# Attention scores with the mask added by TensorE, the maximum subtracted by VectorE, and one exponential per slot

## The chip, the core and the metric

The kernel runs on one core of a Trainium2 chip, as one launch. The metric is the device time in microseconds (us); smaller is better. The engines are TensorE (PE; its weight loads are listed as PEld), VectorE (DVE), ScalarE (ACT), GpSimd (POOL) and SyncE (SP, which issues most of the DMA transfers). They run their own streams in program order and wait for each other by semaphores. TensorE writes its results to PSUM, which VectorE and ScalarE read.

## The reference

The reference chains three parts. The change lies in the first; the other two are only named here.

```python
# attention: q, k, v are (2, 8, 768, 64); blocks of 32, a window of 16
k_sum = k.reshape(B, H, 24, 32, D).max(axis=3)
v_sum = v.reshape(B, H, 24, 32, D).mean(axis=3)
scores_l = scale * q @ k.T                       # kept where |i - j| < 16, else -1e9
scores_s = scale * q @ k_sum.T + log(32)         # 24 summary columns for each row
scores_all = concat([scores_l_masked, scores_s])
a = exp(scores_all - max(scores_all))            # per row
a = a / (sum(a) + 1e-9)
out = a @ concat([v, v_sum])
# then: a mixture of 8 experts (512 -> 1024 -> 512), one expert for each token,
# then: a feed-forward (512 -> 2048 -> 512) with g = h * cos(h)
```

## The kernel before

**Tiles of the attention.** Since the window is narrow, 64 tokens of queries see 96 tokens of keys (KW) and the 24 block summaries: 120 columns (KC) for each tile of 64 tokens. Two heads are worked on together (a pair), and half of the sequence at a time, six tiles: that is a slot. There are 8 pairs (two batches of four) and so 16 slots, numbered i; `p, odd = divmod(i, 2)`. In a slot each of the six tiles gives an array of 128 rows (64 queries of two heads) by 120 columns.

**A slot's work.** `attn_scores` (L255) multiplies on TensorE: the stationary operand is `qz`, in which the queries of the one head stand in rows 0 to 63 and those of the other in rows 64 to 127, in different columns, with zeros in the other two quarters, so that one product of 128 rows gives both heads. It needs `qz` to be cleared once (`clear_qz`) and to be filled in two halves (`prep_q`, L174: one copy on VectorE, one on ScalarE). The six products go to two banks of PSUM (tile `ps`, one buffer). VectorE adds the mask (L269: 0 within the window, -1e9 outside, log 32 on the summaries) into SBUF and takes the negative maximum of each row (L275). In odd slots the means of v for the next pair are also multiplied into a corner of `ps` (L238), and ScalarE copies them out (`evac_v`, L245). `attn_exp` (L278) does six exponentials on ScalarE, each with its own column of maxima as the bias. One slot later `attn_aT` transposes the exponentials on TensorE (L287) and ScalarE copies them to SBUF (L292); another slot later `attn_av` multiplies them with v (L303: half of the array's columns for each tile, 24 instructions), and VectorE divides by the sum (L309, L310, L312).

**What sets the order.** The attention is under a manual schedule: the loop over the slots (`for i in range(NH + 2)`) writes the instructions of all engines in the order in which they are issued, and the loads too (`load_raw` for q, k and v, `load_vw` for the windows of v, all on SP's queue). GpSimd and VectorE reorder the raw rows (`shuffle`, L168) and TensorE transposes them (`prep_k`, L207, with its maxima L215 and copy L198; `prep_q`, L177). Between the slots' pieces stands other work by a plan (`PLAN`, L46, run by `at(i, place)`): the routing of the first batch's tokens to experts (transposes L370 and their copies L373 and L375, logits L382, squares L402, the square root on GpSimd L462, positions and gates), the scatter of the rows to DRAM by expert (L538), the loading of the first window of tokens (L754, x_gate L760, x_first L774) and of the experts' weights. `ON_VECTOR` names copies that VectorE does in place of another engine. After the loop come the experts' windows and the feed-forward (all their products are at L716).

**The start.** The first k, q and v, then the constants `csa` (the mask among them), are loaded on SP's queue; TensorE multiplies zeros meanwhile (`keep_warm`, L1009).

Of the kernel before, what the change touches and what calls it, by code (L numbers as in the profile page):

```python
# [11 lines left out]
F32 = mybir.dt.float32  # L12
# [9 lines left out]
P = 128  # L22
# [39 lines left out]
# patterns times 2**16  # L62
# [3 lines left out]
# column offsets in the constant array  # L66
# [13 lines left out]
def shape_constants():  # L80
# [5 lines left out]
    m = np.zeros((P, NU + 1, KC), np.float32)  # L86
# [3 lines left out]
    m[:, :, :KW] = np.where(band, 0.0, -1e9)[:, None, :]  # L90
    m[:, 0, :WIN] = -1e9
    m[:, NU, KW - WIN:KW] = -1e9
    m[:, :, KW:] = math.log(BLK)
    c[:, C_MASK:C_MASK + (NU + 1) * KC] = m.reshape(P, -1)
# [9 lines left out]
def fused_kernel(ctx, tc, q, k, v, emb, tau, w1, w2, w_in, w_out, consts, out):  # L104
# [6 lines left out]
    # the second batch's rows and transposed rows; later a slot of weights  # L111
# [13 lines left out]
    mask = csa[:, C_MASK - C_VIND:C_TOK - C_VIND]  # L125
# [19 lines left out]
    def load_vw(b, g, half, vw):  # L145
        """the windows of half the sequence; those at its ends are short"""
# [16 lines left out]
    def shuffle(raw, n, scale, ap, eng, r=None):  # L163
        """raw [n, head, token, d] to [n, token, head, d]"""
        if r is None:
            r = ap.tile([P, QJ, 2, D], F32, tag="shuf", name="shuf", bufs=1)
        r = r[0:n]
        eng.tensor_scalar(  # L168
            r.rearrange("p j h d -> p h j d"), raw.rearrange("p h (j d) -> p h j d", d=D),
            scale, 1.0, op0=ALU.mult, op1=ALU.mult,  # L170
        )
        return r

    def prep_q(bf, qs, ps_t):  # L174
        pq = ps_t.tile([P, QJ, P], F32, tag="tr", name="pq")
        for j in range(QJ):
# [11 lines left out]
        tc.declare_no_dep(hi.ins, lo.ins, reason="different quadrants")  # L188
# [13 lines left out]
    def prep_k(bf, kr, pks, ap, eng, copy_first=False):  # L202
        """pks: a tile of PSUM, or two so that two engines can read them"""
# [32 lines left out]
    def prep_v2(va, pv):  # L236
        """the blocks' means of v; pv: 24 partitions of PSUM"""
# [17 lines left out]
    def attn_scores(half, bf, ps_s, ap, va=None):  # L255
        qz, kb = bf["qz"], bf["kb"]
# [19 lines left out]
        return s, nmx, vsm  # L276

    def attn_exp(s, nmx):  # L278
        for u in range(NU):
            nc.scalar.activation(s[:, u, :], s[:, u, :], AF.Exp, bias=nmx[:, u:u + 1])  # L280
# [14 lines left out]
    def attn_av(g, half, aT, bf, xb, ps_s, ap):  # L295
        """half the sequence, two heads"""
# [3 lines left out]
        for u in range(NU):  # L300
            m = 64 * (u % 2)
            for hh in range(2):
                nc.tensor.matmul(  # L303
                    po[m:m + 64, u // 2, hh, :],
                    lhsT=aT[0:KC, u * P + hh * 64:u * P + hh * 64 + 64], rhs=vw[0:KC, hh, u, :],
# [60 lines left out]
    def route_tr(xb, js, xT, pxs):  # L366
        """js: tiles of tokens; pxs: a bank of PSUM for each"""
# [47 lines left out]
    def route_pick(b):  # L415
        """one-hot of each token's expert; L: less its maximum"""
# [1024 lines left out]
```

## Time and profile before

| | us |
|---|---|
| median of 3 runs (538.35 to 541.08) | 539.39 |
| profiled execution, first to last instruction | 535.9 |
| TensorE busy | 507.0 (95%) |
| VectorE busy | 409.2 (76%) |
| ScalarE busy | 305.7 (57%) |
| GpSimd busy | 110.4 (21%) |
| attention, first scores to the experts' first product | 10.9 to 98.3 |

The profiled execution is known by its span alone, 535.9 us; the time of a run is counted around it. TensorE's products are pipelined, and the end of each is modelled, so that its busy share is not its share of the peak: the distance from start to start says more. The share of busy time is a mean over stages with different limits, and the last three quarters of the span are the experts' and the feed-forward's.

### The profile page before, as it was taken

What the parts mean: (1) busy time and instruction counts of PE and PEld (TensorE: products, weight loads), DVE (VectorE), ACT (ScalarE), POOL (GpSimd) and SP (SyncE); (2) the same over time, 40 slices, a digit from 0 to 9 for tenths busy, and PEclk for the clock granted to TensorE, in tenths of its full rate; (3) what the DMA queues carried; (4) which work ended last, traced back from release to release, by engine and by line L of the source; (5) the groups of instructions that cost most, each with busy time, mean ns of one, the idle gap of its engine ahead of it and who ended that gap; (6) DMA issues with size and microseconds to landing.
All of it is one profiled execution on the core that took longest, in us unless ns stands there. A gap on an engine that the chain in (4) does not pass through costs nothing. (4 is left out here: it accounts for less than half of the span.)

```text
span 535.9 us, 9826 instructions
## 1 busy us (share of the span) xinstructions
PE 507.0 (95%) x3556; PEld 464.9 (87%) x3556; DVE 409.2 (76%) x843; ACT 305.7 (57%) x643; POOL 110.4 (21%) x136
## 2 busy tenths in 40 slices
PE   7899986899999999999999999999999999999993
PEld 6788775679999999999999999999999999999992
DVE  5898796897867687889779998976699766655662
ACT  2887775897556566666557675633364433333330
POOL 4777565671524000000000000000000000001222
PEclk8999999999999999999999999999999999999998
DMA  8999848787798556766304333220010000001111
GB/s 219 243 187 255 164 111 269 271 276 245 226 332 264 195 197 206 226 234 199 121 0 153 123 119 118 79 78 1 0 42 2 0 1 0 1 1 60 59 60 64
DMA packets 47688, 72.37 MB, mean 135 GB/s; under 512 B 21256, under 2 KB 21512, under 8 KB 47632
## 3 DMA queue, kind: packets, MB, share of 16 engines
q1 hardware_dynamic: 44800, 62.17, 39.8%
q0 software_dynamic: 2832, 9.49, 5.1%
q8 instruction: 30, 0.49, 0.4%
q14 instruction: 26, 0.21, 0.1%
HBM read 64.28 MB, written 7.37 MB: 134 GB/s over the span
## 5 line engine op out<-in xcount | busy, mean ns | idle before, releaser
L716 PE MATMUL po<-sl,gt 128*128 128x512 f32 x567 | 139.8, 391 | 0.0
L716 PEld LDWEIGHTS po<-sl,gt 128*128 128x128 f32 x567 | 105.6, 188 | 18.2
L716 PE MATMUL ph<-yT,sl 128*128 128x384 f32 x576 | 107.7, 336 | 0.0
L716 PEld LDWEIGHTS ph<-yT,sl 128*128 128x128 f32 x576 | 101.2, 188 | 3.7
L626 DVE TENSOR_TENSOR sl<-raw,sl 128x512 fp32r<-128x512 f32 x112 | 75.0, 705 | 12.5 <-ACT sl L625 12.1
L969 POOL DMA_INDIRECT out_dram<-acc,perm x12 | 12.0, 1000 | 344.6 <-DVE acc L1351 342.2
L625 ACT ACTIVATE sl<-raw 128x512 fp32r<-128x512 f32 x112 | 63.8, 627 | 18.0 <-PE py L716 10.8
L716 PE MATMUL py<-ht,sl 128*128 128x256 f32 x576 | 72.8, 282 | 0.4 <-DVE ht L812 0.4
L716 PE MATMUL ph<-xT,sl 128*128 128x256 f32 x576 | 71.0, 281 | 1.1 <-DVE xT L786 0.8
L716 PEld LDWEIGHTS ph<-xT,sl 128*128 128x128 f32 x576 | 68.4, 188 | 2.5 <-DVE xT L786 1.0
L716 PEld LDWEIGHTS py<-ht,sl 128*128 128x128 f32 x576 | 69.2, 188 | 1.4 <-DVE ht L812 0.8
L926 ACT ACTIVATE u<-u 128x384 f32<-128x384 f32 x64 | 33.6, 525 | 62.8 <-DVE u L925 62.7
L930 ACT ACTIVATE gt<-t 128x384 fp32r<-128x384 f32 x63 | 33.1, 525 | 31.4 <-DVE t L929 31.1
L922 ACT ACTIVATE t<-ph 128x384 f32<-128x384 f32 x64 | 31.3, 489 | 31.5 <-PE ph L716 31.1
L929 DVE TENSOR_TENSOR t<-ph,u 128x384 f32<-128x384 f32 (+1 forms) x66 | 35.7, 543 | 17.7 <-ACT u L926 17.5
L931 DVE TENSOR_TENSOR gt<-t,gt 128x384 fp32r<-128x384 f32 x63 | 35.1, 556 | 17.2 <-ACT gt L930 17.2
L924 DVE TENSOR_SCALAR u<-t 128x384 f32<-128x384 f32 x64 | 22.9, 358 | 27.7 <-ACT t L922 26.8
L925 DVE TENSOR_TENSOR u<-t,u 128x384 f32<-128x384 f32 x64 | 35.5, 555 | 1.1
L716 PE MATMUL ph<-yT,early 128*128 128x384 f32 x192 | 36.1, 338 | 0.2 <-DVE yT L1298 0.2
L716 PEld LDWEIGHTS ph<-yT,early 128*128 128x128 f32 x192 | 33.8, 188 | 1.7 <-DVE yT L1298 0.5
L280 ACT ACTIVATE s<-s,nmx 128x120 f32<-128x120 f32 x96 | 29.0, 383 | 2.0 <-DVE nmx L275 1.3
L260 PE MATMUL ps<-kb,qz 128*128 128x120 f32 x192 | 25.0, 281 | 2.4 <-DVE s L269 1.5
(193 smaller groups left out, 667.7 us busy)
## 6 DMA issues: line engine op xcount, KB each, us to landing
raw<-in_moe_w_dram SPq DMA_DIRECT2D x56, 512.0 KB, 4.6
raw<-in_moe_w_in_dram SPq DMA_DIRECT2D x16, 512.0 KB, 3.7
raw<-in_moe_w_out_dram SPq DMA_DIRECT2D x16, 512.0 KB
vw<-in_v_dram SPq DMA_DIRECT2D x32, 120.0 KB, 4.7
xw<-xs POOLq DMA_DIRECT2D x6, 516.0 KB
kn<-in_k_dram SPq DMA_DIRECT2D x8, 384.0 KB, 4.9
qn<-in_q_dram SPq DMA_DIRECT2D x8, 384.0 KB, 5.7
vn<-in_v_dram SPq DMA_DIRECT2D x8, 384.0 KB, 5.9
```

The costliest lines, as they stand in the source:

```text
L260: nc.tensor.matmul(ps[:, u // 3, (u % 3) * KC:(u % 3) * KC + KC], lhsT=qz[:, t].rearrange("p h s -> p (h s)"), rhs=kb[:, t, :], start=True ...
L280: nc.scalar.activation(s[:, u, :], s[:, u, :], AF.Exp, bias=nmx[:, u:u + 1])
L625: nc.scalar.activation(sl[:, 0, c], r, AF.Copy)
L626: nc.vector.tensor_tensor(sl[:, 1, c], r, sl[:, 0, c].bitcast(F32), op=ALU.subtract)
L716: nc.tensor.matmul(acc, lhsT=lw(a), rhs=lx(c), start=(first and i == 0), stop=(last and i == 2))
L922: nc.scalar.activation(t, ph, AF.Copy, scale=1.0 / TWO_PI, bias=0.25)
L924: nc.vector.tensor_scalar(u, t, ROUND, -ROUND, op0=ALU.add, op1=ALU.add)
L925: nc.vector.tensor_tensor(u, t, u, op=ALU.subtract)
L926: nc.scalar.activation(u, u, AF.Sin, scale=TURN)
L929: nc.vector.tensor_tensor(g, ph[:, cs], u[:, cs], op=ALU.mult)
L930: nc.scalar.activation(gt[:, 0], g, AF.Copy)
L931: lo = nc.vector.tensor_tensor(gt[:, 1], g, gt[:, 0].bitcast(F32), op=ALU.subtract)
```

## The change

The mask goes into PSUM first: TensorE multiplies the identity with the mask (both float32r) and what the rounding of log 32 leaves out, and the scores are accumulated on top. The queries are kept dense (`qT`, no zeros, no clearing), filled by one copy; each product of 64 queries and one head works on a quarter of the array: rows by head, columns by the tile's parity, and the two heads go to different banks. A partition of `ps` therefore belongs to other tokens than before, and the mask needs 4 variants in place of 7. VectorE takes the negative maximum from PSUM and then adds it, into SBUF; one exponential without a bias covers all 720 columns. The copy of q is VectorE's for the first pair and ScalarE's for all others; three copies of transposed rows (x2, x3, x5) go from VectorE to ScalarE; the constants are loaded ahead of v. The mask outside of the window is -2**30.

```diff
-ON_VECTOR = "e2 k4 k6 k8 k12 k14 x2 x3 x5"
+ON_VECTOR = "e2 k4 k6 k8 k12 k14"
+FAR = -2.0 ** 30
-C_TOK = C_MASK + (NU + 1) * KC
+C_TOK = C_MASK + 4 * KC
...
-    def prep_q(bf, qs, ps_t):
+    def prep_q(bf, qs, ps_t, eng):
...
-        qz = bf["qz"]
-        lo = nc.vector.tensor_copy(
-            qz[0:64, :, 0, :].rearrange("d t (s j) -> d t s j", j=QJ),
-            pq[0:64, :, 0:QP].rearrange("d j (t s) -> d t s j", t=NT),
-        )
-        dst = qz[64:128, :, 1, :].rearrange("d t (s j) -> d t s j", j=QJ)
-        src = pq[64:128, :, 0:QP].rearrange("d j (t s) -> d t s j", t=NT)
-        hi = nc.scalar.activation(dst, src, AF.Copy)
+        dst = bf["qT"].rearrange("p (t s j) -> p t s j", t=NT, j=QJ)
+        src = pq[:, :, 0:QP].rearrange("d j (t s) -> d t s j", t=NT)
+        if eng is nc.scalar:
+            nc.scalar.activation(dst, src, AF.Copy)
+        else:
+            eng.tensor_copy(dst, src)
...
     def attn_scores(half, bf, ps_s, ap, va=None):
         ps = ps_s.tile([P, 2, 512], F32, tag="s", name="ps")
-        for u in range(NU):
-            t = NU * half + u
-            nc.tensor.matmul(
-                ps[:, u // 3, (u % 3) * KC:(u % 3) * KC + KC],
-                lhsT=qz[:, t].rearrange("p h s -> p (h s)"), rhs=kb[:, t, :],
-                start=True, stop=True,
-            )
+        for hh in range(2):
+            nc.tensor.matmul(
+                ps[:, hh, 0:3 * KC], lhsT=identr, rhs=maskr[:, half * KC:(half + 3) * KC],
+                start=True, stop=False, skip_group_check=True,
+            )
+            nc.tensor.matmul(
+                ps[:, hh, 0:3 * KC].rearrange("p (u c) -> p u c", u=3)[:, :, KW:KC],
+                lhsT=identr, rhs=masklo.unsqueeze(1).to_broadcast([P, 3, NB]), start=False, stop=False, skip_group_check=True,
+            )
+        for u in range(NU // 2):
+            for hh in range(2):
+                for m in range(2):
+                    t = NU * half + 2 * u + m
+                    hp = slice(64 * hh, 64 * hh + 64)
+                    nc.tensor.matmul(
+                        ps[64 * m:64 * m + 64, hh, u * KC:(u + 1) * KC],
+                        lhsT=qT[hp, t * 64:(t + 1) * 64], rhs=kb[hp, t, :],
+                        start=False, stop=True, skip_group_check=True,
+                    )
         pv = ps[KW:KC, 0, 3 * KC:3 * KC + 2 * D].rearrange("p (h d) -> p h d", h=2)
         if va is not None:
             prep_v2(va, pv)
+        s4 = ps[:, :, 0:3 * KC].rearrange("p a (u c) -> p a u c", u=3)
+        nmx = ap.tile([P, NU], F32, tag="nmx", name="nmx")
+        nc.vector.tensor_reduce(
+            nmx.rearrange("p (a u) -> p a u", a=2), s4, axis=AX.X, op=ALU.max, negate=True
+        )
         s = ap.tile([P, NU, KC], F32, tag="s", name="s")
         nc.vector.tensor_tensor(
-            s.rearrange("p (a u) c -> p a (u c)", a=2), ps[:, :, 0:3 * KC],
-            mask[:, half * KC:(half + NU) * KC].rearrange("p (a c) -> p a c", a=2), op=ALU.add,
+            s.rearrange("p (a u) c -> p a u c", a=2), s4,
+            nmx.rearrange("p (a u) -> p a u", a=2).unsqueeze(3).to_broadcast([P, 2, 3, KC]),
+            op=ALU.add,
         )
         vsm = evac_v(pv, ap) if va is not None else None
-        nmx = ap.tile([P, NU], F32, tag="nmx", name="nmx")
-        nc.vector.tensor_reduce(nmx, s, axis=AX.X, op=ALU.max, negate=True)
...
-        for u in range(NU):
-            nc.scalar.activation(s[:, u, :], s[:, u, :], AF.Exp, bias=nmx[:, u:u + 1])
+        nc.scalar.activation(s, s, AF.Exp)
...
+        maskr = ap1.tile([P, 4 * KC], F32R, name="maskr")
+        masklo = ap1.tile([P, NB], F32R, name="masklo")
+        identr = ap1.tile([P, P], F32R, name="identr")
+        nc.scalar.activation(identr, ident, AF.Copy)
...
         load_raw(*pairs[0], raw, "q")
+        nc.sync.dma_start(csa, consts[:, C_VIND:])
         load_raw(*pairs[0], raw, "v")
-        nc.sync.dma_start(csa, consts[:, C_VIND:])
...
         prep_k(sets[0], kr, two_banks(), ap, nc.gpsimd)
-        prep_q(sets[0], qs, ps_t)
+        prep_q(sets[0], qs, ps_t, nc.vector)
+        nc.scalar.activation(maskr, mask, AF.Copy)
+        nc.gpsimd.tensor_tensor(
+            masklo, mask[:, KW:KC], maskr[:, KW:KC].bitcast(F32), op=ALU.subtract
+        )
```

`attn_av` takes the columns of the transposed exponentials in the new order; every other call of `prep_q` gets `nc.scalar`.

## Rows read from the trace of the kernel before

**Rows 1.** Five stretches: busy us (instructions) of each engine, granted clock, DMA share, GB/s.

```profile
10.90:34.00 23.10, 21.25 (x230) 18.98 (x229) 18.67 (x31) 16.80 (x41) 18.83 (x26) 0.98 1.02 211
34.00:57.00 23.00, 21.25 (x265) 18.06 (x263) 19.53 (x37) 18.80 (x45) 13.72 (x18) 1.00 1.14 244
57.00:78.00 21.00, 18.28 (x205) 15.55 (x205) 17.52 (x48) 16.56 (x44) 13.87 (x16) 1.00 0.61 132
78.00:98.30 20.30, 12.78 (x179) 10.74 (x179) 13.42 (x35) 13.53 (x35) 10.03 (x12) 1.00 0.78 262
98.30:535.90 437.60, 425.81 (x2646) 395.07 (x2646) 333.36 (x683) 236.50 (x479) 49.62 (x44) 0.99 0.36 118
```

**Rows 2.** TensorE's waits, 10.9 to 98.3 us: total us, times, longest.

```profile
PE pk L207 <- POOL shuf L168: 2.2, 3, 1.0
...
PE po L303 <- ACT s L280: 1.8, 2, 1.5
PE ps L260 <- DVE s L269: 1.5, 1, 1.5
```

**Rows 3.** Timeline of TensorE, one slot: start us, us, engine, line.

```profile
47.26 1.52 PE L260 MATMUL ps<-kb,qz 128*128 128x120 f32 x12
48.71 0.97 PE L303 MATMUL po<-vw,aT 120*64 120x65 f32 x24
```

**Rows 4.** Groups by line and form, up to 98.3 us: busy us, mean ns, idle before.

```profile
L260 PE MATMUL ps<-kb,qz 128*128 128x120 f32 x192 | 25.0, 281 | 2.4 <-DVE s L269 1.5 <-issue 0.5 <-POOL qr L168 0.4
...
L269 DVE TENSOR_TENSOR s<-ps,csa 128x720 f32<-128x720 f32 x16 | 14.5, 904 | 8.8 <-PE ps L260 3.7 <-PE ps L238 2.4 <-PE pa L287 2.4
L275 DVE TENSOR_REDUCE nmx<-s 128x6 f32<-128x720 f32 x16 | 14.5, 903 | 0.6
...
L181 DVE COPY qz<-pq 64x768 f32<-64x768 f32 x8 | 7.5, 942 | 0.1
...
L187 ACT ACTIVATE qz<-pq 64x768 f32<-64x768 f32 x8 | 6.5, 808 | 0.2
...
L215 DVE TENSOR_REDUCE ks<-pk 128x24 f32<-128x768 f32 x6 | 5.7, 947 | 1.4 <-PE pk L207 1.2
...
L402 ACT ACTIVATE junk<-xb 128x512 f32<-128x512 f32 x6 | 3.8, 632 | 0.2
```

**Rows 5.** Timeline of TensorE: the routing's logits; six float32r products of the feed-forward.

```profile
56.13 0.85 PE L382 MATMUL pl<-big,enT 128*32 128x384 f32 x8
...
399.59 1.20 PE L716 MATMUL ph<-yT,sl 128*128 128x384 f32 x6
```

**Rows 6.** Timeline of the third slot's beginning, TensorE and VectorE.

```profile
17.87 1.16 PE L1009 MATMUL pw<-still 128*128 128x128 f32 x8 [0.85 <-DVE s L269]
...
18.66 0.94 DVE L181 COPY qz<-pq 64x768 f32<-64x768 f32 x1
...
19.75 1.46 PE L260 MATMUL ps<-kb,qz 128*128 128x120 f32 x11 [0.40 <-POOL qr L168]
```

**Rows 7.** Timeline, 68 to 73 us: from the copy of v's means to the norms.

```profile
68.54 0.27 ACT L245 ACTIVATE vsm<-ps 24x128 f32<-24x128 f32 x1 [0.61 <-DVE s L269]
...
71.22 1.36 POOL L462 TENSOR_TENSOR nm<-nm,half_t 128x6 f32<-128x6 f32 x1 [0.61 <-ACT junk L402]
...
72.61 1.02 DVE L467 TENSOR_SCALAR nm<-nm 128x6 f32<-128x6 f32 x1 [0.51 <-POOL nm L462]
```

**Rows 8.** Timeline, GpSimd's longest wait for k; and a line of the DMA issues.

```profile
56.85 1.05 POOL L168 TENSOR_SCALAR shuf<-kn 100x1024 f32<-100x1024 f32 x1 [4.54 <-DMA kn<-in_k_dram]
...
csa<-in_consts_dram SPq DMA_DIRECT2D x1, 438.0 KB
```

**Rows 9.** Timeline, the attention's tail.

```profile
92.13 1.81 ACT L280 ACTIVATE s<-s,nmx 128x120 f32<-128x120 f32 x6
...
93.55 0.69 POOL L760 TENSOR_SCALAR xw<-xw 128x512 f32<-128x512 f32 x1 [1.71 <-DMA xw<-xs]
...
96.14 0.66 PE L774 MATMUL px<-cst,xw 128*128 128x128 f32 x4
```

More of the change, by code (lines that the diff above doesn't have):

```diff
@@ L85, in shape_constants @@
     c[np.arange(QP), C_VIND + np.arange(QP) // (BLK // QJ)] = 1.0 / BLK
-    m = np.zeros((P, NU + 1, KC), np.float32)
+    m = np.zeros((P, 4, KC), np.float32)
     p = np.arange(P) % 64
@@ L89, in shape_constants @@
     band = np.abs(p[:, None] + WIN - col[None, :]) < WIN
-    m[:, :, :KW] = np.where(band, 0.0, -1e9)[:, None, :]
-    m[:, 0, :WIN] = -1e9
-    m[:, NU, KW - WIN:KW] = -1e9
+    m[:, :, :KW] = np.where(band, 0.0, FAR)[:, None, :]
+    m[0:64, 0, :WIN] = FAR
+    m[64:P, 3, KW - WIN:KW] = FAR
     m[:, :, KW:] = math.log(BLK)
-    c[:, C_MASK:C_MASK + (NU + 1) * KC] = m.reshape(P, -1)
+    c[:, C_MASK:C_MASK + 4 * KC] = m.reshape(P, -1)
     c[:, C_IOTA] = WT * np.arange(P)
@@ L124, in fused_kernel @@
     ones = cst[:, C_ONE:C_ONE + P]
-    mask = csa[:, C_MASK - C_VIND:C_TOK - C_VIND]
     row0 = cst[:, C_IOTA:C_IOTA + 1]
@@ L255, in attn_scores @@
     def attn_scores(half, bf, ps_s, ap, va=None):
-        qz, kb = bf["qz"], bf["kb"]
+        qT, kb = bf["qT"], bf["kb"]
         ps = ps_s.tile([P, 2, 512], F32, tag="s", name="ps")
-        for u in range(NU):
-            t = NU * half + u
+        for hh in range(2):
             nc.tensor.matmul(
-                ps[:, u // 3, (u % 3) * KC:(u % 3) * KC + KC],
-                lhsT=qz[:, t].rearrange("p h s -> p (h s)"), rhs=kb[:, t, :],
-                start=True, stop=True,
-            )
+                ps[:, hh, 0:3 * KC], lhsT=identr, rhs=maskr[:, half * KC:(half + 3) * KC],
+                start=True, stop=False, skip_group_check=True,
+            )
+            nc.tensor.matmul(
[12 more added lines that the diff above has]
+                    )
         pv = ps[KW:KC, 0, 3 * KC:3 * KC + 2 * D].rearrange("p (h d) -> p h d", h=2)
@@ L267, in attn_scores, with attn_exp @@
             prep_v2(va, pv)
+        s4 = ps[:, :, 0:3 * KC].rearrange("p a (u c) -> p a u c", u=3)
[3 more added lines that the diff above has]
+        )
         s = ap.tile([P, NU, KC], F32, tag="s", name="s")
         nc.vector.tensor_tensor(
-            s.rearrange("p (a u) c -> p a (u c)", a=2), ps[:, :, 0:3 * KC],
-            mask[:, half * KC:(half + NU) * KC].rearrange("p (a c) -> p a c", a=2), op=ALU.add,
+            s.rearrange("p (a u) c -> p a u c", a=2), s4,
+            nmx.rearrange("p (a u) -> p a u", a=2).unsqueeze(3).to_broadcast([P, 2, 3, KC]),
+            op=ALU.add,
         )
         vsm = evac_v(pv, ap) if va is not None else None
-        nmx = ap.tile([P, NU], F32, tag="nmx", name="nmx")
-        nc.vector.tensor_reduce(nmx, s, axis=AX.X, op=ALU.max, negate=True)
-        return s, nmx, vsm
-    def attn_exp(s, nmx):
-        for u in range(NU):
-            nc.scalar.activation(s[:, u, :], s[:, u, :], AF.Exp, bias=nmx[:, u:u + 1])
+        return s, vsm
+    def attn_exp(s):
+        nc.scalar.activation(s, s, AF.Exp)
     on_vector = set(ON_VECTOR.split())
@@ L304, in attn_av @@
                     po[m:m + 64, u // 2, hh, :],
-                    lhsT=aT[0:KC, u * P + hh * 64:u * P + hh * 64 + 64], rhs=vw[0:KC, hh, u, :],
+                    lhsT=aT[0:KC, (3 * hh + u // 2) * P + m:(3 * hh + u // 2) * P + m + 64], rhs=vw[0:KC, hh, u, :],
                     start=True, stop=True,
@@ L1018, in fused_kernel @@
                 vw=[ap1.tile([P, 2, NU, D + 1], F32, name=f"vw{i}{h}") for h in range(2)],
-                qz=ap1.tile([P, NT, 2, 64], F32, name=f"qz{i}"),
+                qT=ap1.tile([P, S], F32, name=f"qT{i}"),
                 kb=ap1.tile([P, NT, KC], F32, name=f"kb{i}"),
@@ L1022, in fused_kernel @@
             sets.append(s)
-        def clear_qz(s, eng):
-            eng.memset(s["qz"][64:128, :, 0, :], 0.0)
-            eng.memset(s["qz"][0:64, :, 1, :], 0.0)
         def clear_vw(s):
@@ L1031, in clear_vw @@
                 nc.gpsimd.memset(vw[:, :, :, D:D + 1], 1.0)
-        clear_qz(sets[0], nc.vector)
         nc.gpsimd.memset(half_t, 0.5)
@@ L1039, in fused_kernel @@
         clear_vw(sets[0])
-        clear_qz(sets[1], nc.gpsimd)
         clear_vw(sets[1])
@@ L1071, in fused_kernel @@
         prep_k(sets[0], kr, two_banks(), ap, nc.gpsimd)
-        prep_q(sets[0], qs, ps_t)
+        prep_q(sets[0], qs, ps_t, nc.vector)
+        mask = csa[:, C_MASK - C_VIND:C_TOK - C_VIND]
+        nc.scalar.activation(maskr, mask, AF.Copy)
+        nc.gpsimd.tensor_tensor(
+            masklo, mask[:, KW:KC], maskr[:, KW:KC].bitcast(F32), op=ALU.subtract
+        )
         keep_warm(6, P)
@@ L1195, in fused_kernel @@
             elif nx is not None and odd and i > 1:
-                prep_q(nx, qs, ps_t)
+                prep_q(nx, qs, ps_t, nc.scalar)
             at(i, "p")
@@ L1200, in fused_kernel @@
             if i < NH:
-                s, nmx, vsm = attn_scores(
+                s, vsm = attn_scores(
                     odd, sets[p % 2], ps_s, ap, va if nx is not None and odd and i > 1 else None
@@ L1211, in fused_kernel @@
             if i == 1:
-                prep_q(nx, qs1, ps_t)
+                prep_q(nx, qs1, ps_t, nc.scalar)
             if i == 2:
@@ L1227, in fused_kernel @@
             if i < NH:
-                attn_exp(s, nmx)
+                attn_exp(s)
             if nx is not None and not odd and i and i not in EARLY:
```

1 line of the change is left out of this document (removed).

## The prediction

> **What bounds the kernel now.** I read the stretches first [rows 1]. The attention runs from 10.9 to 98.3 us of a span of 535.9, and the change touches only what lies before 98.3; from there TensorE is busy 425.8 of 437.6 us on work that stays as it is. So the question is by how much the first product of the experts, which opens that last stretch, moves. In the attention no engine is alone at the limit. From 10.9 to 34.0 TensorE is busy 21.3 of 23.1 us, VectorE 18.7, GpSimd 18.8, and the DMA share is 1.02. From 34.0 to 57.0 the DMA share is 1.14: the loads of q, k and v set the pace beside TensorE. From 57.0 to 78.0 DMA falls to 0.61 and VectorE and ScalarE carry the first batch's routing between the slots; from 78.0 to 98.3 TensorE is busy only 12.8 of 20.3 us, so chains of latency rule. The list of waits says it from TensorE's side [rows 2]: it waits 2.2 us in all for GpSimd's shuffles of k, 1.8 us for exponentials and 1.5 us, once, for the scores' PSUM. ScalarE, which the change relieves most, is the releaser of little.
>
> **The change part by part.** Durations come from the profiled execution, whose span is 535.9 us; the median of the runs shown is 539.39, so 3.5 us lie around the span, and I forecast the difference and add it to the median.
>
> *Scores on TensorE.* Now a slot has 12 instructions (two to a product), and from the first to the first of the next group it takes 48.71 - 47.26 = 1.45 us [rows 3]. With 281 ns for the last one [rows 4], the other eleven starts are (1.52 - 0.28) / 11 = 0.113 us apart. From the last start (48.50) to the group behind it, which uses half the array's columns, are 0.20 us: a switch of shape costs about 0.09 more than a step. After the change: two mask products of 360 columns in float32r, two of 72 columns, then 24 instructions on quarters. Six float32r instructions of 384 columns take 1.20 us with the last one's length in it, so a mask is at most 0.20; I take 0.17 [rows 5]. The small ones lie between 0.03 (72 of 384 columns of that) and 0.113 (a step with its weight load of 128 columns); I take 0.07. One more switch, 0.09. For the quarters the nearest row is that of the routing's logits: 8 instructions of 384 columns, on four column groups, take 0.85 us in all [rows 5]; one after the other at the scores' pace (0.113 for 120 columns) they would take 2.9. So four column groups run together. That groups of rows do so too no row shows. Bounds: four together, 6 x 0.113 = 0.68 us; two together, 1.36; one by one, 2.71. I take 0.68, nearest to the row on groups. Sum: 0.34 + 0.14 + 0.09 + 0.68 + 0.09 = 1.34 us, that is 0.11 less than now; with the bounds 0.6 more (pairs) or 1.9 more (one by one).
>
> The Trainium skill (TensorE: Matmul & The Clock Gate, Part 3, Packing small matmuls) says that row and column groups compose, with 10.6 times measured on sixteen tiles; for columns the trace agrees (0.85 us), for rows no run here shows it, and by it the 0.68 stands.
>
> The Trainium skill (TensorEngine Tiling (Array Packing), Key Properties) speaks against the change: a switch of tiling mode drains TensorE. The 0.09 us above agrees; by the rule, too, each slot pays one drain more.
>
> *Maximum and subtraction on VectorE.* Now the mask's addition takes 904 ns and the maximum 903 [rows 4]. The maximum is now read from PSUM: the reduction of 768 elements from there takes 947, so about 0.90 for 720; the subtraction has the addition's shape. No change in busy time (bounds: 0.1 us either way). What changes is the order: the scores' PSUM is free only after both, 0.9 us later than now. That shows where TensorE waits for it: at 17.87 it waited for the addition of the slot before [rows 6], so that row comes 0.9 later; 0.3 of it comes back because the scores at 19.75 stood behind VectorE's copy of q (18.66 to 19.60), which ScalarE now does earlier. +0.6 us, once. In the later slots TensorE waited once for that addition [rows 2]; elsewhere the next scores come later than it, and the 0.9 costs between nothing and 0.5 us a slot (behind the waiting scores stand the transposes and products of the slots before, in order). I take nothing, since the busy row of 10.9 to 34.0 shows TensorE with other work in between.
>
> *One exponential.* Six instructions take 1.81 us [rows 9]. One of 720 columns: 632 ns for 512 [rows 4], 0.83 ns a column beyond, about 0.81. ScalarE saves 1.0 us a slot, 16 us in all, hidden except where it ends last.
>
> *Copies.* VectorE loses q's half copy (942 ns, seven of eight times); ScalarE's copy over 128 partitions has the 768 elements of now (808). Three copies of x go from VectorE to ScalarE, into the time that the exponentials leave.
>
> *Start.* The constants come ahead of v and shrink from 438 KB [rows 8] by three masks of 120 columns, 184 KB; at 211 GB/s [rows 1] that is 0.9 us of DMA. The queue is full then, but I count half, -0.4, since v is needed before the constants' end would have been. The mask's rounding (a copy on ScalarE, a small subtraction on GpSimd) stands behind k's copies, and TensorE does its warming products until the first scores at 10.9 us: nothing, but up to 0.5 us if the constants land after 10 us, for the whole queue of TensorE stands behind the first mask. The clearing of q's zero halves falls while engines wait for k: nothing.
>
> *Where it adds up.* **Up to 34 us**: +0.6 (PSUM held), -0.7 (six slots of 0.11 at full TensorE), -0.4 (constants): -0.5. **34 to 57**: TensorE's 0.11 and ScalarE's second end in waits for loads; GpSimd waits 4.54 us for k at 56.85 [rows 8], and that load's end is set by the full DMA. 0 (bounds -0.9, +0.5). **57 to 98.3**: two things against each other. The mean of v is copied out of the scores' bank by ScalarE only when VectorE has left it [rows 7]: 68.54 now, 0.8 later after the change, and behind it stand the squares, GpSimd's power and VectorE's 72.61, thus the routing's positions and its scatter: up to +0.8. In the tail each slot's exponential is 1.0 us shorter in a chain (92.13, then transposes, copy and product) that ends at 96.14, while the tokens are ready at 93.55 + 0.69 = 94.24 [rows 9]; the held PSUM gives 0.9 of one slot back there. Between -1.9 and +0.8; I take -0.3. **Sum: -0.8 us**, 539.4 - 0.8 = 538.6.
>
> **The rivals.**
> *The relief comes through.* Each slot after 57 us is shorter by a part of ScalarE's 1.0 and VectorE's 0.94. For it: the 1.8 us that TensorE waits for exponentials [rows 2], and 7.5 idle us in the tail. Against it: the copy of v's mean waits longer. It gains the 1.8, the 1.9 at the tail's end, and 0.9 of the 2.2 us for shuffles, with nothing lost at the start: -4.6, 534.8.
> *The quarters run in pairs only* (columns together, rows in turn), the case on the other side. Place: the scores of every slot; price 0.68 us more each; it decides from the first slot on, since TensorE is full up to 34 us. Six slots give 4.1, the five up to 57 (3.4) vanish in the waits for loads, the rest give about 1: -0.8 + 5.1, 543.7. For it: only column groups are seen together. Against it: nothing in those is lost; the 24 instructions of 65 columns on two groups take 0.97 us [rows 3], and one after the other, at 0.113 for 120 columns, 1.47.
> *One by one.* 2.03 us more a slot: 12.2, 6.8 and about 5: some 562. Against it: the same rows.
>
> **How the numbers follow.** The sum near nothing 0.52, its own range 536.0 to 541.2; the relief 0.24; pairs 0.16; one by one 0.08. A change of 0.5% (2.7 us) is about what a measurement here tells from none. Faster: the relief and 0.06 of the first, 0.30. Slower: 0.04 of the first, 0.13 of the pairs, and one by one: 0.25. Same: 0.45. The range goes from 533.0 (the relief with a little more) to 544.5 (pairs) and leaves out one by one and the tails, some 0.13.
>
> **What would show it.** Right: the quarters' instructions in six rounds about 0.11 apart and 1.3 us from a slot's first mask to the next group; the maximum near 0.90 and the exponential near 0.81 us; the copy of v's mean 0.8 later behind the scores; the experts' first product near 97.5. Wrong: that product before 95 (the relief), rounds of two, or TensorE waiting for VectorE's subtraction in most slots, which would add up to 0.5 us each.

## The result, and the profile after

The changed kernel is slower: 546.17 us (544.01 to 547.47) against 540.24 for the one before, run beside it, a ratio of 1.0102 [1.0067, 1.0136] (in brackets 95% intervals, here and below); in a second set of runs it was 1.0110 [1.0072, 1.0148]. That is 5.9 us where I forecast -0.8. The profiled span grew from 535.9 to 542.0 us, and the experts' first product, by which the whole forecast was reckoned, moved from 98.31 to 103.91. Two slow runs far from their neighbours (546.05 us with the means first and x back, 1267.62 us in the old order with x back) are in no ratio below.

First the stretches of the kernel after, bounds moved with the slots (columns as in [rows 1]).

```profile
10.90:34.60 23.70, 21.17 (x316) 17.77 (x319) 17.69 (x28) 12.57 (x19) 18.23 (x25) 0.98 1.10 224
34.60:59.40 24.80, 21.59 (x345) 17.40 (x336) 18.27 (x33) 13.90 (x23) 16.59 (x22) 1.00 1.02 238
59.40:80.50 21.10, 18.08 (x273) 14.77 (x269) 15.71 (x45) 14.43 (x29) 11.35 (x14) 1.00 0.40 97
80.50:103.90 23.40, 15.93 (x211) 12.97 (x211) 12.83 (x34) 9.16 (x16) 13.41 (x16) 0.85 0.68 228
103.90:542.00 438.10, 426.43 (x2646) 395.85 (x2646) 331.49 (x683) 236.42 (x479) 43.37 (x40) 0.99 0.36 117
```

The last stretch is that of [rows 1] (438.1 us for 437.6): 5.6 of the 6.1 us were lost before it. In the attention VectorE and ScalarE have less to do than before (64.5 and 50.1 us over the four rows for 69.1 and 65.7), yet the stretch is 5.6 us longer. So the two that the change relieves did not hold it up by their work; something became later. The starts of the slots' scores say where, in us:

| slot | 5 | 6 | 7 | 10 | 12 | 13 | 14 | 15 | experts |
|---|---|---|---|---|---|---|---|---|---|
| before | 32.96 | 38.14 | 42.20 | 60.56 | 70.18 | 75.46 | 81.19 | 87.77 | 98.31 |
| after | 33.63 | 38.02 | 44.24 | 61.94 | 71.54 | 77.93 | 83.76 | 91.47 | 103.91 |
| later by | 0.67 | -0.12 | 2.04 | 1.38 | 1.36 | 2.47 | 2.57 | 3.70 | 5.60 |

On VectorE and ScalarE the parts themselves cost what I said (the mask products did not; see below). Groups by line and form of the kernel after: busy us, mean ns of one, idle before.

```profile
L260 PE MATMUL ps<-maskr,identr 128*128 128x360 f32 x32 | 11.9, 436 | 4.1 <-DVE s L287 1.7 <-DVE rs L325 1.7 <-issue 0.6
L273 PE MATMUL ps<-kb,qT 64*64 64x120 f32 x384 | 14.2, 280 | 0.0
L283 DVE TENSOR_REDUCE nmx<-ps 128x6 f32<-128x720 f32 x16 | 14.4, 903 | 16.6 <-PE ps L273 7.5 <-PE ps L237 5.3 <-remote 3.8
L287 DVE TENSOR_TENSOR s<-ps,nmx 128x720 f32<-128x720 f32 x16 | 14.5, 908 | 1.2
L296 ACT ACTIVATE s<-s 128x720 f32<-128x720 f32 x16 | 12.8, 798 | 2.7 <-DVE s L287 2.7
```

Maximum 0.90, subtraction 0.91, exponential 0.80. TensorE's list of waits, too, looks harmless: for the scores' tile it waits in four slots, 3.4 us in all (before: once, 1.5).

```profile
PE po L319 <- issue: 3.2, 4, 1.2
PE ps L260 <- DVE s L287: 1.7, 2, 0.9
PE ps L260 <- DVE rs L325: 1.7, 2, 1.2
```

The change of place shows on ScalarE. Its waits ahead of the copy of v's means out of the scores' tile, in the kernel before:

```profile
ACT vsm L245 <- PE pv L238: 3.1, 1, 3.1
ACT vsm L245 <- DVE s L269: 3.0, 4, 1.1
```

and in the kernel after:

```profile
ACT vsm L244 <- DVE rs L325: 9.8, 4, 2.8
ACT vsm L244 <- DVE s L287: 4.8, 2, 2.4
```

The loop copies the means in six slots, the odd ones from 3 to 13 (the row on `pv` is the set-up's copy ahead of it). ScalarE stands idle there for 14.6 us in all six, where it was 3.0 in four. Measured from the slot's first score, the copy is 0.91, 0.62, 0.52, 1.16, 0.99 and 0.10 us later than before, 4.3 us in all; the rest of the longer idle time is ScalarE being ready sooner, with its shorter exponentials. One of these waits in the timeline of the kernel after (start us, us, engine, line; brackets: the idle time before it):

```profile
46.10 0.91 DVE L283 TENSOR_REDUCE nmx<-ps 128x6 f32<-128x720 f32 x1 [1.01 <-PE ps L237]
46.89 0.87 PE L303 MATMUL pa<-cst,s 128*120 128x128 f32 x6
47.11 0.91 DVE L287 TENSOR_TENSOR s<-ps,nmx 128x720 f32<-128x720 f32 x1
48.11 0.27 ACT L244 ACTIVATE vsm<-ps 24x128 f32<-24x128 f32 x1 [2.48 <-DVE rs L325]
48.41 0.81 ACT L308 ACTIVATE aT<-pa 120x768 f32<-120x768 f32 x1
48.43 0.19 PEld L260 LDWEIGHTS ps<-maskr,identr 128*128 128x128 f32 x1 [0.18 <-ACT vsm L244]
48.54 1.65 POOL L249 TENSOR_SCALAR vw<-vsm 24x768 f32<-24x768 f32 x2 [3.51 <-ACT vsm L244]
```

The means are read after both of VectorE's instructions (48.02 is the subtraction's end). Both engines only read the tile; no run tried the copy without that order. Behind the copy stand the next aT copy, which could have begun at the transposes' end (47.76), GpSimd's 3.51 us of idle time before it writes the means into the windows, and TensorE's next mask. In slot 11 the norms of the routing stand behind it. The slot's first score before, and the timeline after:

```profile
65.73 1.50 PE L260 MATMUL ps<-kb,qz 128*128 128x120 f32 x12
```

```profile
67.15 0.41 PE L260 MATMUL ps<-maskr,identr 128*128 128x360 f32 x1
70.95 0.27 ACT L244 ACTIVATE vsm<-ps 24x128 f32<-24x128 f32 x1 [2.78 <-DVE rs L325]
71.25 0.63 ACT L418 ACTIVATE junk<-xb 128x512 f32<-128x512 f32 x1
73.51 0.81 ACT L308 ACTIVATE aT<-pa 120x768 f32<-120x768 f32 x1
73.63 1.36 POOL L478 TENSOR_TENSOR nm<-nm,half_t 128x6 f32<-128x6 f32 x1 [0.62 <-ACT junk L418]
74.37 0.97 PE L319 MATMUL po<-vw,aT 120*64 120x65 f32 x24 [1.07 <-ACT aT L308]
75.02 1.03 DVE L483 TENSOR_SCALAR nm<-nm 128x6 f32<-128x6 f32 x1 [1.40 <-POOL nm L478]
75.95 0.90 DVE L283 TENSOR_REDUCE nmx<-ps 128x6 f32<-128x720 f32 x1
76.88 0.91 DVE L287 TENSOR_TENSOR s<-ps,nmx 128x720 f32<-128x720 f32 x1
77.93 0.40 PE L260 MATMUL ps<-maskr,identr 128*128 128x360 f32 x1 [0.90 <-DVE s L287]
```

From the slot's first score to the means' copy are 3.80 us, and 6.48 to the power; before they were 2.81 and 5.49 ([rows 7]). The squares go ahead of aT, and TensorE waits 1.07 for that. VectorE waits 1.40 for the power, with slot 12's maximum behind it in order, and slot 13's first mask then waits 0.90 for the subtraction. By that the lateness grows by 1.1 us from slot 12 to slot 13.

The largest step in the table is not the copy alone: from slot 6 to slot 7 the lateness grows by 2.16 us. Ahead of slot 6's maximum VectorE has two small instructions on SBUF that take longer than before: one 1.22 us for 0.56, the other 1.41 for 0.31. The second one, in the kernel before:

```profile
39.43 0.31 DVE L223 TENSOR_SCALAR kb<-ks 128x288 f32<-128x288 f32 x1
```

and after, with what GpSimd does beside it:

```profile
40.91 1.26 POOL L230 TENSOR_TENSOR va<-vn 96x512 f32<-96x512 f32 x1
40.93 1.41 DVE L222 TENSOR_SCALAR kb<-ks 128x288 f32<-128x288 f32 x1
44.24 0.40 PE L260 MATMUL ps<-maskr,identr 128*128 128x360 f32 x1 [1.18 <-DVE rs L325]
```

The maximum starts at 42.26, the subtraction ends at 44.10, and slot 7's first mask waits for that. In the kernel before GpSimd stood idle at 39.43, waiting for q's load. The other two traces of the changed kernel (again, and x back) have the same 1.2 and 1.41 us; that GpSimd's work is the cause is not shown.

### The profile page after: what moved, and what is told of

The parts are those of the page before. It is cut to its first block, busy times and chain, and to the rows that moved or that the text cites. A ratio compares the mean times of both kernels' runs of the same rounds, so it can differ in the third digit from the quotient of the medians.

```text
span 542.0 us, 10261 instructions
## 1 busy us (share of the span) xinstructions
PE 510.8 (94%) x3812; PEld 465.2 (86%) x3812; DVE 401.3 (74%) x831; ACT 289.8 (53%) x567; POOL 105.9 (20%) x135
## 5 line engine op out<-in xcount | busy, mean ns | idle before, releaser
L732 PEld LDWEIGHTS po<-sl,gt 128*128 128x128 f32 x567 | 105.6, 188 | 18.2
L642 DVE TENSOR_TENSOR sl<-raw,sl 128x512 fp32r<-128x512 f32 x112 | 73.3, 691 | 12.2 <-ACT sl L641 11.9
L283 DVE TENSOR_REDUCE nmx<-ps 128x6 f32<-128x720 f32 x16 | 14.4, 903 | 16.6 <-PE ps L273 7.5
L828 DVE SCALAR_TENSOR_TENSOR ht<-ph,ht 128x256 fp32r<-128x256 f32 x48 | 20.2, 420 | 8.7 <-ACT ht L827 7.8
```

The lines of the kernel that those rows point to most:

```text
L283: nc.vector.tensor_reduce(nmx.rearrange("p (a u) -> p a u", a=2), s4, axis=AX.X, op=ALU.max, negate=True)
L642: nc.vector.tensor_tensor(sl[:, 1, c], r, sl[:, 0, c].bitcast(F32), op=ALU.subtract)
L732: nc.tensor.matmul(acc, lhsT=lw(a), rhs=lx(c), start=(first and i == 0), stop=(last and i == 2))
L828: nc.vector.scalar_tensor_tensor(ht[:, 1], ph, 0.0, ht[:, 0].bitcast(F32), op0=ALU.max, op1=ALU.subtract)
```

## The experiments

Theory 1: it is the order in which the scores' tile is read (held through two instructions of VectorE, the means' copy behind both). Theory 2: the new instructions of TensorE cost it. Theory 3: the half clock that the changed kernel shows near the end of the attention, or the three copies of x on ScalarE. Ratios to the kernel before on the same chip, with 95% intervals; "half clock" is the time that TensorE ran at half of its clock, reckoned from a run's mean as 2 x (1 - granted clock) x span, in us, as a mean over the runs (before: 10 to 12); "experts" is the start of their first product in the profile. It differs by up to 2.3 us between two profiles of one kernel, so the ratios decide.

| kernel | ratio | half clock | experts |
|---|---|---|---|
| changed, again | 1.0110 [1.0072, 1.0148] | 17.8 | 106.0 |
| changed, x back on VectorE | 1.0112 [1.0065, 1.0159] | 19.4 | 107.2 |
| means first | 1.0039 [1.0015, 1.0062] | 16.1 | 99.3 |
| means first, x back | 1.0016 [0.9987, 1.0044]; 1.0013 [0.9990, 1.0036] | 15.7; 15.9 | 100.4; 102.5 |
| old order | 1.0052 [1.0031, 1.0073] | 15.8 | 102.0 |
| old order, x back | 1.0026 [0.9997, 1.0055]; 1.0026 [1.0010, 1.0041] | 15.7; 13.8 | 98.1 |
| the same, masks twice | 1.0060 [1.0035, 1.0084] | 12.1 | 103.7 |
| quarters alone | 0.9967 [0.9940, 0.9995]; 0.9974 [0.9947, 1.0002] | 20.3; 18.2 | 99.7; 97.4 |
| before, maximum first | 1.0076 [1.0048, 1.0103] | 11.7 | 102.8 |
| changed, no maximum | 1.0213 [1.0185, 1.0241] | 18.4 | 111.2 |
| quarters alone, means first | 1.0040 [1.0014, 1.0067] | 21.9 | 98.1 |
| quarters alone, fillers | 1.0059 [1.0033, 1.0085] | 14.6 | 99.9 |
| both of these | 1.0158 [1.0121, 1.0194] | 17.8 | 106.2 |

**The old order of VectorE and ScalarE, TensorE's part kept.**

```diff
-        nc.vector.tensor_reduce(
-            nmx.rearrange("p (a u) -> p a u", a=2), s4, axis=AX.X, op=ALU.max, negate=True
-        )
...
-        nc.vector.tensor_tensor(
-            s.rearrange("p (a u) c -> p a u c", a=2), s4,
-            nmx.rearrange("p (a u) -> p a u", a=2).unsqueeze(3).to_broadcast([P, 2, 3, KC]),
-            op=ALU.add,
-        )
+        nc.vector.tensor_copy(s.rearrange("p (a u) c -> p a u c", a=2), s4)
         vsm = evac_v(pv, ap) if va is not None else None
+        nc.vector.tensor_reduce(nmx, s, axis=AX.X, op=ALU.max, negate=True)
...
-        nc.scalar.activation(s, s, AF.Exp)
+        for u in range(NU):
+            nc.scalar.activation(s[:, u, :], s[:, u, :], AF.Exp, bias=nmx[:, u:u + 1])
```

> The changed kernel with its TensorE part (mask products, dense queries, quarters) kept and the old order of VectorE and ScalarE put back: VectorE first copies the masked scores out of PSUM (about 0.85 us, as the old addition did), then takes the maximum from SBUF, and six exponentials carry the maximum as their bias. Theory 1, the scores' one PSUM tile is held some 0.9 us longer because two instructions in a row read it there, and the copy of v's means, which reads the same tile, comes later, so that the routing of the tail is late: the time goes back to 540 +/- 2 us, the scores of slot 13 start near 75.5 us as before and not at 77.9, and TensorE's wait for VectorE's second reader is gone. Theory 2, TensorE's new instructions and the switches between them cost it: the time stays at 544 us or more. Theory 3, three copies of x that went from VectorE to ScalarE and the half clock near the end cost it: 544 to 546 us, too, and the half clock at 90 to 97 us stays.

Half of the loss is gone, not all. With the copies of x back on VectorE as well:

> The changed kernel's TensorE part (mask products and quarters) with VectorE's and ScalarE's old order, and the copies of x on VectorE too: against quarters alone (0.997) it differs only by the four mask products of a slot, against the changed kernel with x back (1.011) only by the order of VectorE and ScalarE. Theory 1: the order is nearly all of it, 1.000 to 1.003. Theory 2: the mask products are, 1.005 to 1.010; 16 slots by 0.55 us are 9 us of TensorE, of which a third shows.

1.0026: theory 1's figure; the order is worth 1.0112 - 1.0026 = 0.86%, 4.6 us (from two sets of runs; their intervals leave 0.3 to 1.4%).

**The means' copy first**, which undoes only the second half of theory 1; VectorE still holds the tile through both instructions.

```diff
+        vsm = evac_v(pv, ap) if va is not None else None
         nc.vector.tensor_reduce(
...
-        vsm = evac_v(pv, ap) if va is not None else None
```

> The changed kernel with one thing moved: ScalarE's copy of v's means comes ahead of the maximum in the order in which the scores' PSUM tile is read. Theory 1 (in the form that the routing is late by the means' copy): the power of the norms in slot 12 starts 1 to 1.5 us earlier than in the changed kernel (73.6 us), the first scatter too, and the time falls by about 1.5 us to 544.5. In the form that the scores' tile is held too long: the maximum is now behind a copy on ScalarE in the even slots, and the time stays or rises by up to 1 us. Theories 2 and 3: no difference, 546 us.

The power started 4.0 us earlier than in the changed kernel, not 1 to 1.5 (2.1 of it because slot 11 itself began earlier), and the time fell by 0.6 to 0.7%, more than I expected. Its slot 11, to be laid beside the one above:

```profile
65.07 0.41 PE L260 MATMUL ps<-maskr,identr 128*128 128x360 f32 x1
66.93 0.27 ACT L244 ACTIVATE vsm<-ps 24x128 f32<-24x128 f32 x1 [0.76 <-PE ps L237]
67.23 0.91 DVE L284 TENSOR_REDUCE nmx<-ps 128x6 f32<-128x720 f32 x1 [0.27 <-ACT vsm L244]
69.48 0.81 ACT L308 ACTIVATE aT<-pa 120x768 f32<-120x768 f32 x1
69.61 1.36 POOL L478 TENSOR_TENSOR nm<-nm,half_t 128x6 f32<-128x6 f32 x1 [0.62 <-ACT junk L418]
```

1.86 us from the scores to the means and 4.54 to the power, for 3.80 and 6.48. It costs VectorE 0.27. With the copies of x (slots 2, 3 and 5) on VectorE again, in both kernels:

```diff
-ON_VECTOR = "e2 k4 k6 k8 k12 k14"
+ON_VECTOR = "e2 k4 k6 k8 k12 k14 x2 x3 x5"
```

> The changed kernel with the three copies of x (slots 2, 3 and 5 of the list) back on VectorE. If their place costs (TensorE waited 1.1 us for ScalarE's copy at 57.8 us in the changed kernel): 1 us faster than the changed kernel run beside it. If they were moved because VectorE is the longer chain after the change: 0 to 1.5 us slower. Theory 1 says nothing of them beyond that VectorE's 0.9 us a slot is what the hold is made of, so slower is likelier.

> The changed kernel with the copy of v's means ahead of the maximum (worth some 3.5 us so far) and also with the three copies of x back on VectorE. Theory 1: the rest between that kernel and the one before (2 us) is not from the copies of x, so 538 to 541 us. If the copies of x are the rest: 536 to 538 us.

> The changed kernel itself, unaltered, on the same chip as the three others, so that they can be compared with it directly: 1.010 of the kernel before, as in its first runs, 543 to 546 us; mean half-clock time of 16 to 17 us a run.

The copies' place makes no difference that these runs can tell (1.0112 for 1.0110, to some 0.6%). With the means first the changed kernel is as fast as with the old order (1.0016 and 1.0013 for 1.0026 twice): what the order cost comes back when the means' copy alone is moved. That the longer hold by itself costs nothing is not shown, for the two also differ by the shorter exponentials, which may pay for it. One stretch shows the hold: from slot 11's scores to slot 13's it is 9.73 us in the kernel before, 9.66 and 9.67 in the two with masks and the old order, 10.25 to 10.26 in three traces with the means first, and 10.78 in all three of the changed kernel: there about half of the loss is the hold's and half the late copy's.

**The same order in the kernel before.** Here the maximum lacks the mask.

```diff
+        nc.vector.tensor_reduce(
+            nmx.rearrange("p (a u) -> p a u", a=2),
+            ps[:, :, 0:3 * KC].rearrange("p a (u c) -> p a u c", u=3),
+            axis=AX.X, op=ALU.max, negate=True,
+        )
...
         vsm = evac_v(pv, ap) if va is not None else None
-        nc.vector.tensor_reduce(nmx, s, axis=AX.X, op=ALU.max, negate=True)
```

> The kernel before with one thing changed: the maximum is taken from the scores in PSUM ahead of the addition of the mask (so it is the maximum without the mask), then the addition reads the same tile. VectorE has as many instructions as before, of the same sizes; only the tile is held some 0.9 us longer and v's means are copied later. Theory 1: slower than the kernel before by 3 to 5 us, 543 to 545 us, with TensorE waiting for VectorE's second reader and the scores of slot 13 later than 75.5 us. Theories 2 and 3: no difference from the kernel before, 540 us.

1.0076: 4.1 us, with nothing else changed, no quarters and 0.9 us of half clock more than the kernel before beside it. Hold and late copy come together here, too. ScalarE's waits ahead of the means' copy:

```profile
ACT vsm L245 <- DVE rs L313: 5.7, 4, 1.9
ACT vsm L245 <- DVE s L275: 3.4, 2, 2.0
```

**No maximum.**

Both instructions of VectorE on the scores go, and:

```diff
-        nc.scalar.activation(s, s, AF.Exp)
+        nc.scalar.activation(s.rearrange("p (a u) c -> p a u c", a=2), s4, AF.Exp)
```

> The changed kernel with the maximum and its subtraction left out: one exponential for a slot reads the masked scores directly in PSUM, so that VectorE has about 1.8 us less in each of 16 slots, and the tile is read once, for 0.8 us. Theory 1 (PSUM held and VectorE's chain): 535 to 538 us, below the kernel before. Theory 2 (TensorE's new instructions): not under 543 us. Theory 3 (half clock near the end): between them, 540 to 543 us, with the stall at 85 to 90 us and the half clock after it still there.

Theories 1 and 3 missed; theory 2's bound (not under 543 us) is met, but by another way than its own: with 29 us less on VectorE it is the slowest of all, and TensorE's instructions are those of the changed kernel. Its timeline shows why.

```profile
28.43 0.85 PE L273 MATMUL ps<-kb,qT 64*64 64x120 f32 x24
31.34 0.81 ACT L300 ACTIVATE aT<-pa 120x768 f32<-120x768 f32 x1 [1.35 <-PE pa L295]
32.05 0.77 ACT L288 ACTIVATE s<-ps 128x720 f32<-128x720 f32 x1
32.87 0.43 PE L260 MATMUL ps<-maskr,identr 128*128 128x360 f32 x1 [0.87 <-ACT s L288]
```

The exponential, now the tile's reader, stands on ScalarE behind the copy of the slot before, for which transposes had to run: the tile is let go 3.5 us after the scores were there, and TensorE waits for it in 11 slots, 14.0 us in all. I had counted how long its reader takes (0.8) and not where it stands. Here it is the hold itself that costs, since the means' copy no longer waits for VectorE's two instructions.

**Quarters alone**, without mask products and in the old order, the mask added by VectorE, x on VectorE. The dense queries, their one copy and the earlier constants come with the quarters.

The four mask products go, the exponentials are the six of the old order, and against the changed kernel:

```diff
-                        start=False, stop=True, skip_group_check=True,
+                        start=True, stop=True,
...
         nc.vector.tensor_tensor(
-            s.rearrange("p (a u) c -> p a u c", a=2), s4,
-            nmx.rearrange("p (a u) -> p a u", a=2).unsqueeze(3).to_broadcast([P, 2, 3, KC]),
+            s.rearrange("p (a u) c -> p a (u c)", a=2), ps[:, :, 0:3 * KC],
+            mask[:, half * KC:(half + 3) * KC].unsqueeze(1).to_broadcast([P, 2, 3 * KC]),
             op=ALU.add,
         )
         vsm = evac_v(pv, ap) if va is not None else None
+        nc.vector.tensor_reduce(nmx, s, axis=AX.X, op=ALU.max, negate=True)
```

> Dense queries and scores on quarters alone, without the rest of the change: no mask products; VectorE adds the mask while it takes the scores out of PSUM, takes the maximum from SBUF, six exponentials with a bias, and the copies of x stay on VectorE as in the kernel before. The scores' tile is held as briefly as before; TensorE has about 0.55 us less in each slot than before. Theory 1 (only the longer hold and the late copy of v's means cost the changed kernel): no slower than before and up to 4 us faster, 534 to 538 us, with slot 13's scores at 74 to 75.5 us. Theory 3 (quarters bring another 5 us of half clock into the attention's last slots, as in all three kernels with quarters so far: mean half-clock time 16 us a run against 11 without quarters): the stretch is there, and it takes 1.5 us back, 537 to 539 us.

Faster than the kernel before by 1.4 to 1.8 us on two chips, the only version that is (the second interval just touches 1). A slot's scores, first to the next group, take 0.78 us:

```profile
48.90 0.84 PE L264 MATMUL ps<-kb,qT 64*64 64x120 f32 x24
49.68 0.56 PE L309 MATMUL po<-vw,aT 120*64 120x65 f32 x10
```

**The mask products**, by doubling them, with quarters alone, one set, and the means first beside it on one chip.

```diff
-        for hh in range(2):
+        for hh in (0, 1, 0, 1):
             nc.tensor.matmul(
```

> Quarters with masks and VectorE's and ScalarE's old order (1.003 of the kernel before), the mask products of every slot issued twice (the second set starts the sums anew, so the values are the same): another 0.55 us of TensorE in each of 16 slots. Theory 2 (mask products show in the time): 2 to 5 us slower than with one set, run beside it, 1.007 to 1.012. Theory 1 (TensorE has room in the slots, only the order of readers counts): 0 to 1 us slower, 1.003 to 1.005.

> Quarters alone, unaltered from its first runs (0.997), for comparison on this chip. If a set of mask products costs what doubling it shows, this one is faster than the kernel with one set by the same amount; 0.996 to 1.000 of the kernel before.

> Quarters with one set of mask products, VectorE's and ScalarE's old order, copies of x on VectorE: unaltered from its first runs (1.003). 1.001 to 1.005 of the kernel before.

> The changed kernel with the means' copy first and the copies of x on VectorE, unaltered from its first runs (1.002). Theory 1: within 0.3% of the kernel in the old order beside it, 1.000 to 1.005 of the kernel before, though VectorE still holds the tile through two instructions: what the hold cost in the changed kernel, it cost through the means' copy.

A second set adds 0.34% (1.8 us; the intervals leave 0.05 to 0.63%), the first adds 0.52% over quarters alone (2.8 us; 0.2 to 0.8%), of some 9 us of TensorE each. VectorE's copy that takes the place of the mask's addition lasts as long (902 ns for 904). 1.0060 lies between what theory 1 (to 1.005) and theory 2 (from 1.007) had said; that the masks cost something holds, so TensorE had less room in the slots than theory 1 said.

**The means first with quarters alone, and products meant to hold the clock.** The line of the means' copy, moved up, is the one edit, the loop (4, 6, 4 and 4 products in slots 12 to 15) the other; they were tried each by itself and both together.

```diff
+        vsm = evac_v(pv, ap) if va is not None else None
         nmx = ap.tile([P, NU], F32, tag="nmx", name="nmx")
...
-        vsm = evac_v(pv, ap) if va is not None else None
+        for _ in range(fill):
+            nc.tensor.matmul(
+                ps[:, 1, 3 * KC:512], lhsT=ident, rhs=cst[:, 0:512 - 3 * KC], start=True, stop=True,
+            )
         nc.vector.tensor_reduce(nmx, s, axis=AX.X, op=ALU.max, negate=True)
```

> Quarters alone (the kernel that was 0.997 of the one before) with the copy of v's means ahead of VectorE's addition. Theory 1: the means' copy heads the chain to the routing of the last slots, so 0.3 to 0.8 us earlier there and 0 to 1 us faster than without: 0.995 to 0.998 of the kernel before. Rival (the half clock near the end takes back whatever comes earlier): no difference, 0.997.

> Quarters alone with products that compute nothing of use (152 columns each into the unused columns of the scores' tile; 4, 6, 4 and 4 of them in slots 12 to 15, after the addition) so that TensorE isn't idle while it waits there. Theory 3: the half clock from 78 to 92 us goes away or shrinks (mean half-clock time from 20 us a run to 10 to 13), and the time falls by 1 to 2 us against the kernel without them, to 0.993 to 0.995 of the kernel before. Rival: the half clock lies where TensorE waits anyway, or the fillers are in the way of the next products: no difference or up to 1 us slower, 0.997 to 0.999.

> Both of the two above: quarters alone, the means' copy first, and the products of no use in slots 12 to 15. If both gains are real and add up: 0.991 to 0.994 of the kernel before, 534 to 535 us. If neither is: 0.997 to 0.999.

None came as hoped. Where the means' copy already stood behind one instruction only, to put it first gained nothing and lost 0.7% (against quarters alone on the two other chips; they did not run beside it); its profile doesn't show where, and that stays open. The fillers lowered the half clock (20.3 and 18.2 to 14.6) but wrote the scores' tile and so waited for VectorE, with the queue behind them:

```profile
67.06 0.85 PE L264 MATMUL ps<-kb,qT 64*64 64x120 f32 x24
70.70 0.90 DVE L274 TENSOR_TENSOR s<-ps,csa 128x720 f32<-128x720 f32 x1
71.65 1.47 PE L281 MATMUL ps<-cst 128*128 128x152 f32 x8 [3.48 <-DVE s L274]
```

What the half clock costs is not answered by them (an estimate from all runs stands under the tail, below).

## Why the prediction was wrong

*Scores on TensorE: right in mechanism, 0.08 us a slot too low.* The products on quarters run four together: the 24 instructions start within 0.583 us, 0.10 to a round (0.68 forecast). By the Trainium skill (TensorE: Matmul & The Clock Gate, Part 3, Packing small matmuls) row and column groups compose; this trace agrees: the four of a round start within 0.02 us. The rivals of pairs and of one by one are out. The masks were dearer: a mask to the next small product 0.24 (0.17 forecast), small to quarters 0.13. A slot's block takes 1.42 us for 1.45 before, not 1.34, so the 0.7 us up to 34 were not there. Nor were the 0.4 for the constants (the first score at 10.95 us for 10.92); the 0.6 for the held tile were (slots 2 to 5 are 0.6 to 0.8 later; at slot 6 that is gone).

*What the masks cost, and the quarters give, was netted too early.* Quarters alone (with the dense queries and the start) are worth -0.3%, the masks +0.5%: as the slots hang on TensorE in part, the two belong in the sum one by one, about -1.6 and +2.8 us.

*The held tile: the step that failed.* I wrote that the means' copy comes 0.8 us later, named the squares, the power and the scatter behind it, and then set up to +0.8 for it against the shorter exponentials, once, in the stretch from 57 us. The size for one slot was right (0.99 in slot 11). Wrong was to let it count once and to let it be paid: it is in six slots, 4.3 us in all, on an engine that works in order, so that the aT copy behind it, GpSimd's write of the means (11.1 us of idle time ahead of it for 4.1) and TensorE's next mask take it up, and the 1.0 us that the exponential saves comes after the subtraction on that same engine, which then stands waiting. The hold itself I set at nothing beyond the start; TensorE waited 1.18, 0.90 and 0.52 us for it in slots 7, 13 and 15 (before: 1.53 in slot 15 alone). I looked for it on TensorE's list of waits, where it shows in four slots of 16; my sign for wrong, a wait for the subtraction in most slots, did not come, and the loss came all the same. The path was another, too. I had it end at the tokens, by way of positions and scatter, but they lay ready 5.0 us before the product that takes them (before: 1.9):

```profile
96.03 0.69 POOL L776 TENSOR_SCALAR xw<-xw 128x512 f32<-128x512 f32 x1 [1.12 <-DMA xw<-xs]
101.74 0.66 PE L790 MATMUL px<-cst,xw 128*128 128x128 f32 x4
```

The lateness came through the slots instead, as from 12 to 13. By the forecast's stretches: up to slot 5 +0.7 (forecast -0.5), to slot 10 +0.7 (forecast 0), from there +4.2 (forecast -0.3). The runs: the order costs +0.86%, 4.6 us; put back, or the means alone put first, it is gone; put into the kernel before, it costs 4.1. Not all of the 4.2 us is followed through the trace slot by slot.

*The relief.* ScalarE's 16 us (exponentials 12.8 for 29.0) and VectorE's copies of q (1.0 for 7.5) are saved as forecast, and the attention did not get shorter by them: that rival's 4.6 us are out. What the one exponential is worth by itself no run shows.

*The tail.* The half clock was not in the forecast. In the changed kernel TensorE is busy 3.34 of the 6.3 us before 90.3 (within one group of products it pauses for 1.21 and 1.17 us, and the profile names no releaser), and then the granted clock is 0.50:

```profile
84.00:90.30 6.30, 3.34 (x56) 2.73 (x56) 1.66 (x4) 1.24 (x2) 3.18 (x4) 1.00 0.82 268
90.30:97.10 6.80, 6.28 (x63) 5.14 (x61) 4.38 (x10) 1.50 (x2) 3.87 (x5) 0.50 0.94 307
```

That is 1.2 of 2.4 GHz. In it slot 15's scores, products and transposes take 1.48, 1.62 and 1.54 us where 0.85, 0.97 and 0.87 are usual: at most some 2 us of this trace's 5.6. But quarters alone have as much of it over their runs as the changed kernel and are faster than the kernel before, and the kernel before with the maximum first has 0.9 us more of it than without and loses 4.1 us. So it is not the main cause. What it is worth can be estimated from the runs: within one kernel and set, over the 266 runs that count in the table, a run with 1 us more of half clock took 0.22 us longer. By that the 8 us more of the changed kernel (17.8 for 9.7) go with some 1.7 of its 5.9 us; it is an estimate, and which comes first it does not say.

The sum as measured: -1.6 (quarters) + 2.8 (masks) + 4.6 (order) = 5.8, for 5.9. That it comes out is no check: each term is the difference of neighbours in one row of kernels, from the one before to the changed one with x back, so that they add up to its 1.0112 whatever they are. Each is known to between 1 and 3 us.

## What to carry to other kernels

When a step keeps a buffer longer, list every reader of it on every engine, and for each what stands behind it in its engine's order; price it in every slot in which it occurs, and look for it as idle time of that engine, not only in the waits of the engine that fills the buffer. Release a shared PSUM tile with the instruction that comes first, or put the short reader of another engine ahead of the long ones; where one instruction let the tile go already, that gained nothing here. An engine's saved busy time gains nothing where its next instruction waits for the step that got longer.

## What the runs showed of the hardware that I had not expected

On one chip the half clock grew as TensorE's work in the slots shrank: 12.1 us a run with masks twice, 13.8 with one set, 18.2 with quarters alone (12.2 before). TensorE's work is not all of it: the changed kernel, with one set, has 17.8 on another chip. The kernel before itself had medians from 536.4 to 540.2 us on five sets of runs: only ratios to the kernel before beside it compare. And two profiles of the unaltered changed kernel differ: in the second TensorE waits 1.8 us for GpSimd's shuffle of k near 29 us, in the first it doesn't, as in some profiles of other versions; 2 us in the middle of one profile are not yet an effect.
